# Moving TensorE's bias additions ahead in its written order, and fewer zero products between them

## The chip, the cores and the metric

The kernel runs on one core of one Trainium2 chip. A core has five engines that run side by side and meet only at semaphores: TensorE (PE in the profile) multiplies matrices, VectorE (DVE) and ScalarE (ACT) work elementwise, GpSimd (POOL) issues most of the loads here, and SyncE (SP) issues stores and a few loads. TensorE writes into PSUM, which this kernel uses as four "pairs" of two banks each. The metric is the time of one execution on the device in microseconds (us), as a median over runs.

## The reference

There are 8 batches of 576 tokens. The first part is attention with 8 heads of 64, a window of 128 tokens and a linear distance bias per head; the second mixes tokens with a small hypernetwork.

```python
scores = scale * np.matmul(q, k.transpose(0, 1, 3, 2))
bias = slopes[:, None, None] * (-np.abs(rel).astype(np.float32))[None, :, :]
mask = (rel >= 0) & (rel < window)
scores = np.where(mask, scores + bias[None], -1000000000.0)
attn = np.exp(scores - np.max(scores, axis=-1, keepdims=True))
attn = attn / (np.sum(attn, axis=-1, keepdims=True) + 1e-09)
x = np.matmul(attn, v)            # heads side by side: 576 x 512 a batch
wq, wk = x @ w_q, x @ w_k         # 576 x 64 each
W_tok = scale * np.einsum('bsd,btd->bst', wq, wk)
mixed = np.einsum('bst,btd->bsd', W_tok, x)
out = np.maximum(mixed, 0.0) @ w_out
```

## The kernel before

**Tiles.** A batch has four groups of key blocks (128 tokens each; the last group also takes the tail of 64), and each group two units `u` of four heads. Batches are handled in pairs from the mixing stage on.

**Names.** The work is cut into named operations, each with its batch and part:

- `Lq`, `Lk`, `Lv`, `Lt`: loads by GpSimd of a block of 128 tokens of q, k or v, or of the tails of two batches (lines 387 to 402). `LF` loads the first blocks on other queues. `Lw` and `Lwo` load the weights on SyncE (lines 449 to 461), behind `wz`, a small memset on VectorE (line 447).
- `TQ` (`TF`, `TJ` in batch 0): TensorE transposes a block of q and k into PSUM. `ETQ`, `EF`, `EJ` copy it out. `TT` and `ETT` do the tails.
- `QK`: scores of one group and unit into one pair, products over 64 rows. `EXP`: ScalarE's exponential of that pair into SBUF (line 613).
- `BI`: two products over 128 rows that write the logarithmic bias, mask included, into the pair, onto which `QK` then adds. This is so for the twelve units of batches 0 and 1, groups 0 to 2 (`PEB`). For the others `MUL` multiplies the exponentials by the exponential of the bias on VectorE (line 620).
- `PV`: exponentials times values, with the row sums. `RC` and `X`: VectorE's reciprocal and normalisation (lines 677 and 663). `XT`: transposes of the result.
- `WK`, `WQ`, `WT`, `G`, `MX`, `OUT`: the mixing stage and the output products; `EO` and `DO` copy and store.
- `WM.i`: `WARM[i]` products of zeros by zeros (128 x 128 by 128 x 256) into a bank that nobody reads. They have no effect on the output.

**Order.** The order of all work is one written list, `ORDER`. A word such as `BI0.2.0:P1` gives operation, engine and place in PSUM: P is TensorE, A ScalarE, D VectorE, G GpSimd, S SyncE; `P1` is pair 1 whole, `P01` bank 1 of pair 0. Each engine works through its words in their order. Dependencies and the reuse of buffers and banks become semaphore waits. So an operation that waits holds up all that stands behind it on its engine. The unit's bias is the operation that takes the pair; the scores follow into the same pair, and the exponential frees it:

```python
        if added:
            own = add("BI", b, f"{g}.{u}", w - 0.5, pe(0.43), [mkg[u], idh], eb, banks=2)
            s = add("QK", b, f"{g}.{u}", w, pe(0.225), [own, *need], em, mode=1)
        x = add("EXP", b, f"{g}.{u}", w + 0.6, {"ACT": (0.92, 1.02)}, [s, *oldp], ex, frees=[own])
```

The numbers in these calls are notes of the list's making; they play no part when the list is followed.

Of the kernel before, what the change touches and what calls it, by code (L numbers as in the profile page):

```python
# [47 lines left out]
WARM = (13, 3, 3, 8, 12, 2, 1, 8, 4, 11, 4, 3, 5, 5, 2, 2, 3)  # L48
# [4 lines left out]
WM.1:P10 TF0.1.0:P01 EF0.0.0:D TF0.0.1:P20 EF0.1.0:A WM.2:P10 Lq0.3:G ones:D EF0.0.1:A  # L53
TF0.1.1:P21 BI0.0.0:P1 EF0.1.1:A BI0.0.1:P3 Lk1.3:G QK0.0.0:P QK0.0.1:P EXP0.0.0:A TJ0.1.1:P20
TJ0.2.0:P21 Lq1.3:G EXP0.0.1:A WM.3:P10 Lk0.2:G EJ0.2.0:D zeros:D EJ0.1.1:A BI0.1.0:P0 Lk1.2:G
BI0.1.1:P1 QK0.1.0:P biasl:D QK0.1.1:P TT0:P20 Lq1.2:G EXP0.1.1:A TJ0.3.0:P21 WM.4:P30 Lk0.3:G
EXP0.1.0:A ETT0:D EJ0.3.0:D Lk1.1:G ETT1:D TQ1.3:P00 WM.5:P30 Lq1.1:G ETQ1.3:D TJ0.2.1:P01
WM.6:P10 EJ0.2.1:D BI0.2.1:P3 Lv0.1:G QK1.3.1:P2 BI0.2.0:P1 QK0.2.1:P EXP1.3.1:A QK0.2.0:P
QK1.3.0:P0 Lv0.0:G EXP1.3.0:A MUL1.3.1:D TQ1.2:P20 Lq1.0:G WM.7:P21 ETQ1.2:D EXP0.2.1:A Lv0.2:G
MUL1.3.0:D BI1.2.1:P0 TJ0.3.1:P20 EXP0.2.0:A QK1.2.1:P Lk1.0:G EJ0.3.1:D WM.8:P30 EXP1.2.1:A  # L60
QK0.3.1:P2 BI1.2.0:P3 Lv0.3:G QK0.3.0:P1 QK1.2.0:P EXP0.3.1:A TQ1.1:P00 Lk2.1:G WM.9:P01
ETQ1.1:D EXP0.3.0:A Lq2.1:G MUL0.3.1:D EXP1.2.0:A PV0.1:P1 Lv1.2:G MUL0.3.0:D BI1.1.0:P2
BI1.1.1:P0 QK1.1.0:P RC0.1:D QK1.1.1:P Lv1.3:G X0.1:D EXP1.1.0:A PV0.0:P3 RC0.0:D PV0.2:P1
Lk2.2:G X0.0:D EXP1.1.1:A WM.10:P20 RC0.2:D Lv1.1:G X0.2:D PV0.3:P3 WM.11:P20 RC0.3:D Lq2.2:G
TQ1.0:P10 X0.3:D XT0.0:P11 ETQ1.0:A Lk2.3:G TQ2.1:P30 EXT0.0:D XT0.1:P31 Lq2.3:G WM.12:P20
EXT0.1:A PV1.3:P1 Lv1.0:G BI1.0.0:P2 BI1.0.1:P0 QK1.0.0:P RC1.3:D QK1.0.1:P Lk2.0:G X1.3:D
WM.13:P31 EXP1.0.1:A ETQ2.1:D PV1.2:P1 Lv1.4:G EXP1.0.0:A WM.14:P31 RC1.2:D Lq2.0:G wz:D
TQ2.2:P00 X1.2:D Lw:S WM.15:P31 ETQ2.2:D Lv0.4:G XT1.1:P01 Lwo.2:S Lwo.0:S WM.16:P31 EXT1.1:D
Lt1:G Lwo.1:S TQ2.3:P00 Lwo.3:S QK2.1.1:P1 ETQ2.3:D PV1.0:P2 EXP2.1.1:A PV1.1:P3 RC1.0:D Lk3.3:G
X1.0:D QK2.2.1:P0 QK2.2.0:P1 EXP2.2.1:A RC1.1:D Lq3.3:G X1.1:D PV1.4:P2 EXP2.2.0:A XT1.0:P30  # L70
RC1.4:D Lk3.0:G X1.4:D TQ2.0:P31 EXT1.0:A Lq3.0:G PV0.4:P0 ETQ2.0:D QK2.1.0:P1 CWQ:A Lk3.1:G
RC0.4:D QK2.0.1:P2 X0.4:D QK2.0.0:P3 EXP2.0.1:A Lq3.1:G MUL2.1.1:D XTT0:P00 WK0:P01 CW.2:A
EXTT0:D Lk3.2:G MUL2.2.0:D EXP2.0.0:A WT0:P00 pads:D WQ0:P20 EWK0:A EWT0:D EXP2.1.0:A CW.0:D
Lq3.2:G G0:P21 EWQ0:D CW.1:D TT2:P30 EG0:A MUL2.2.1:D Lt2:G ETT2:D MX0.0:P0 MX0.2:P1 RM0.0:A
RM1.0:D MX0.1:P2 RM1.1:A CW.3:D MX0.3:P0 RM0.1:A TQ3.3:P31 Lv2.3:G RM1.3:D RM0.3:A QK2.3.0:P2
# [96 lines left out]
def kernel(  # L172
# [55 lines left out]
    def two(bank):  # L228
        return pairs[bank[0]]
# [748 lines left out]
```

## Time and profile before

| | us |
|---|---|
| median of 3 runs (143.6 to 144.33) | 143.62 |
| the profiled execution | 143.94 |
| its span, first to last instruction | 142.2 |
| TensorE busy | 135.0 |
| ScalarE busy | 116.3 |
| VectorE busy | 113.8 |
| GpSimd busy | 95.6 |

TensorE's 89 zero products are counted in its busy time. Busy times of matmuls overlap, since they are pipelined. The lines that the prediction shows are copied from the profile: an instruction line gives its start, its length, engine, source line, operation, what it writes and reads, how many, and in square brackets the idle time before it with what ended it. All matmuls stand at lines 250 and 253, which are helpers, so the tiles tell them apart: `warm` is a zero product, `blog,identh` a bias, `qkT` scores, `identh,nat` a transpose of q and k, `vt,pt` a `PV`.

### The profile page before, as it was taken

Reading aid. Unit: us, or ns where it says so; the run is one execution under the profiler, and the core shown is the slowest. Engines: PE = TensorE matmul, PEld = TensorE weight load, DVE = VectorE, ACT = ScalarE, POOL = GpSimd, SP = SyncE. Lnnn points to the kernel's source line nnn. Section 1 sums busy time; section 2 is a strip of 40 time slices with the busy share of each in tenths; the row PEclk is TensorE's granted clock in tenths of the full one; section 3 lists DMA queues with packets and bytes.
Section 4 is the critical chain, followed back from the end, with each engine's and each line's share of the span. In section 5 each row is a group of like instructions: output and inputs, shape, how many; then the busy total and the mean of one; then the engine's idle time right before and its main releaser. Section 6 shows DMA issues by size and latency. Waiting matters only on the chain.

```text
span 142.2 us, 4683 instructions
## 1 busy us (share of the span) xinstructions
PE 135.0 (95%) x1933; PEld 91.1 (64%) x1933; DVE 113.8 (80%) x269; ACT 116.3 (82%) x165; POOL 95.6 (67%) x118
## 2 busy tenths in 40 slices
PE   7999999999998999999999999999999999999980
PEld 5857657877763654689855448678765658763440
DVE  4976547766899999999879999999999999737240
ACT  4875496654997899999999999999999997968530
POOL 7999999999948969999989469999660000000000
PEclk9999999999999999999999999999999999999999
DMA  4999999999999999999999999999999955312694
GB/s 100 202 142 143 151 150 153 154 156 151 208 275 154 157 157 154 155 192 157 236 157 222 292 163 154 200 157 186 262 181 155 331 203 231 142 74 52 183 360 150
DMA packets 119478, 25.60 MB, mean 180 GB/s; under 512 B 114209, under 2 KB 114465, under 8 KB 119457
## 3 DMA queue, kind: packets, MB, share of 16 engines
q0 software_dynamic: 109264, 13.77, 152.9%
q1 hardware_dynamic: 9136, 11.28, 23.7%
q10 hardware_dynamic: 1056, 0.26, 0.8%
q8 instruction: 15, 0.25, 0.7%
q14 instruction: 7, 0.05, 0.1%
HBM read 29.62 MB, written 9.44 MB: 275 GB/s over the span
## 4 chain that ended last, share of the span: by engine, by line
PE 75%; ACT 14%; DVE 5%; issue 3%; DVEq 0%; ACTq 0%
PE pair L250 60%; PE pair L253 16%; ACT pt L613 10%; ACT rm L810 2%; DVE x L663 1%; DVE qkT L259 1%; DVE osb L259 1%; ACT wqT L257 1%; ACT xT L257 1%; DVE inv L677 1%; DVE xtl L663 0%; ACT gs L257 0%; ACT wkt L257 0%; DVE xTt L259 0%; DVE warm L300 0%
## 5 line engine op out<-in xcount | busy, mean ns | idle before, releaser
L613 ACT ACTIVATE pt<-pair 128x1024 f16<-128x1024 f32 x64 | 62.2, 1036 | 10.0 <-PE pair L250 9.8
L401 POOL DMA_DIRECT2D vt<-in_v_dram x40 | 35.1, 911 | 6.4 <-DMA nat<-in_q_dram 3.1
L250 PE MATMUL pair<-wout_sb,rm 128*128 128x512 f16 (+1 forms) x132 | 31.2, 373 | 0.0
L388 POOL DMA_DIRECT2D nat<-in_k_dram x31 | 29.6, 962 | 1.1 <-PE pair L253 1.1
L388 POOL DMA_DIRECT2D nat<-in_q_dram x30 | 29.0, 973 | 1.0 <-DMA nat<-in_k_dram 0.7
L620 DVE TENSOR_TENSOR pt<-pt,bias 128x1024 f16<-128x1024 f16 x36 | 23.6, 685 | 0.6 <-ACT pt L613 0.5
L250 PEld LDWEIGHTS <-pt 128*128 128x128 f16 x576 | 20.9, 97 | 4.0 <-issue 1.2
L250 PE MATMUL pair<-vt,pt 128*128 128x65 f16 x576 | 22.8, 193 | 0.0
L663 DVE TENSOR_TENSOR x<-pair,inv 128x512 f16<-128x512 f32 x32 | 21.8, 688 | 0.8
L250 PE MATMUL pair<-qkT 64*128 64x256 f16 (+2 forms) x320 | 21.0, 250 | 0.0
L259 DVE COPY qkT<-pair 128x1024 f16<-128x1024 f16 (+1 forms) x29 | 16.6, 593 | 5.2 <-PE pair L253 4.9
L250 PEld LDWEIGHTS <-rm 128*128 128x128 f16 x132 | 11.5, 98 | 12.3 <-issue 1.3
L253 PE MATMUL pair<-identh,nat 128*128 128x128 f16 x244 | 18.5, 219 | 0.1
L250 PEld LDWEIGHTS <-qkT 64*128 64x128 f16 x320 | 11.0, 94 | 9.8 <-issue 4.6
L257 ACT COPY osb<-pair 128x512 f32<-128x512 f32 x26 | 14.7, 622 | 3.0 <-PE pair L250 3.0
L253 PEld LDWEIGHTS <-nat 128*128 128x128 f16 x244 | 14.6, 98 | 3.3 <-issue 1.9
L250 PE MATMUL pair<-warm 128*128 128x256 f16 x89 | 14.2, 299 | 1.5 <-DVE warm L300 1.1
L259 DVE COPY osb<-pair 128x512 f32<-128x512 f32 (+1 forms) x11 | 7.1, 641 | 6.8 <-PE pair L250 6.1
L257 ACT COPY xT<-pair 128x1024 f16<-128x1024 f16 x11 | 10.9, 1013 | 1.9 <-PE pair L253 1.9
L620 DVE TENSOR_TENSOR pt<-pt,biasl 128x1024 f16<-128x1024 f16 x16 | 10.6, 687 | 1.4 <-ACT pt L613 1.3
L257 ACT COPY qkT<-pair 128x1024 f16<-128x1024 f16 (+1 forms) x12 | 10.7, 925 | 1.2 <-PE pair L253 1.2
L250 PEld LDWEIGHTS <-warm 128*128 128x128 f16 x89 | 8.8, 106 | 3.4 <-DVE warm L300 1.1
(71 smaller groups left out, 154.3 us busy)
## 6 DMA issues: line engine op xcount, KB each, us to landing
out_dram<-osb SPq DMA_DIRECT2D x31, 256.0 KB, 3.2
vt<-in_v_dram POOLq DMA_DIRECT2D x32, 128.0 KB, 6.4
nat<-in_k_dram POOLq DMA_DIRECT2D x31, 128.0 KB, 5.8
nat<-in_q_dram POOLq DMA_DIRECT2D x30, 128.0 KB, 6.1
out_dram<-osb SPq DMA_DIRECT2D x10, 128.0 KB, 2.6
osb<-in_moe_w_out_dram SPq DMA_DIRECT2D x4, 256.0 KB, 6.5
osb<-in_q_dram SPq DMA_DIRECT2D x4, 128.0 KB, 3.2
natt<-in_q_dram POOLq DMA_DIRECT2D x4, 128.0 KB, 5.5
```

Of the source, the lines that this page charges most:

```text
L250: hold(nc.tensor.matmul(*a, **k))
L253: hold(nc.tensor.transpose(*a))
L257: hold(nc.scalar.copy(out_ap, in_ap))
L259: hold(nc.vector.tensor_copy(out=out_ap, in_=in_ap))
L388: return lambda: nc.gpsimd.dma_start(out=natv(b, j, n), in_=(q, k)[j][b, :, P * n:P * n + P, :].transpose([1, 0, 2]))
L401: return lambda: nc.gpsimd.dma_start(out=vtv(b, t)[:n, :, 0:D], in_=v[b, :, P * t:P * t + n, :].transpose([1, 0, 2]))
L613: nc.scalar.activation(out=pt[:, 0:1024], in_=two(own.bank).rearrange("p e c -> p (e c)"), func=AF.Exp, scale=SCALE)
L620: ENG2[o.eng].tensor_tensor(out=pt[:, 0:1024], in0=pt[:, 0:1024], in1=bt, op=ALU.mult)
L663: nc.vector.tensor_tensor(out=x[r].rearrange("p (g h d) -> p g h d", g=2, h=4), in0=sums(p)[r, :, :, 0:64], in1=box["inv"][r].unsqueeze(3) ...
L677: nc.vector.reciprocal(out=box["inv"][r], in_=sums(p)[r, :, :, 64])
L810: hold(nc.scalar.activation(out=out_ap, in_=in_ap, func=AF.Relu, scale=WSCALE))
```

## The change

The words of all engines but TensorE keep their order. In TensorE's list, within batches 0 and 1:

- `BI0.0.0` goes from behind the first transposes' end to the place right behind `TF0.0.0`; `BI0.2.1` and `BI0.2.0` go ahead of `TQ1.3`; `BI1.2.0` ahead of `QK0.3.1`; `BI1.1.0` and `BI1.1.1` ahead of `PV0.1`; `BI1.0.0` ahead of `PV0.3`; `BI1.0.1` ahead of `PV1.3`.
- The zero products go from 89 in 17 groups to 44 in 12 groups, and a new operation `WA.0` adds two zero products onto the pair that holds `BI0.2.1`, because every pair or bank is in use there.

The order on TensorE from the start to the second batch's first scores, with the number of zero products behind each `WM` and `WA`:

```
before: WMx13 TF0.0.0 WMx3 TF0.1.0 TF0.0.1 WMx3 TF0.1.1 BI0.0.0 BI0.0.1 QK0.0.0 QK0.0.1 TJ0.1.1 TJ0.2.0
  WMx8 BI0.1.0 BI0.1.1 QK0.1.0 QK0.1.1 TT0 TJ0.3.0 WMx12 TQ1.3 WMx2 TJ0.2.1 WMx1 BI0.2.1 QK1.3.1 BI0.2.0
  QK0.2.1 QK0.2.0 QK1.3.0 TQ1.2 WMx8 BI1.2.1 TJ0.3.1 QK1.2.1 WMx4 QK0.3.1 BI1.2.0 QK0.3.0 QK1.2.0 TQ1.1
  WMx11 PV0.1 BI1.1.0 BI1.1.1 QK1.1.0 QK1.1.1 PV0.0 PV0.2 WMx4 PV0.3 WMx3 TQ1.0 XT0.0 TQ2.1 XT0.1 WMx5
  PV1.3 BI1.0.0 BI1.0.1 QK1.0.0 QK1.0.1 WMx5 PV1.2 WMx2 TQ2.2 WMx2 XT1.1 WMx3 TQ2.3 (from here the same)
after:  WMx13 TF0.0.0 WMx1 BI0.0.0 TF0.1.0 TF0.0.1 WMx3 TF0.1.1 BI0.0.1 QK0.0.0 QK0.0.1 TJ0.1.1 TJ0.2.0
  WMx3 BI0.1.0 BI0.1.1 QK0.1.0 QK0.1.1 TT0 TJ0.3.0 BI0.2.1 BI0.2.0 TQ1.3 WMx2 TJ0.2.1 WAx2 QK1.3.1
  QK0.2.1 QK0.2.0 QK1.3.0 TQ1.2 WMx4 BI1.2.1 TJ0.3.1 QK1.2.1 BI1.2.0 QK0.3.1 QK0.3.0 QK1.2.0 TQ1.1
  WMx3 BI1.1.0 BI1.1.1 PV0.1 QK1.1.0 QK1.1.1 PV0.0 PV0.2 BI1.0.0 PV0.3 WMx3 TQ1.0 XT0.0 TQ2.1 XT0.1
  BI1.0.1 PV1.3 QK1.0.0 QK1.0.1 WMx5 PV1.2 WMx2 TQ2.2 WMx2 XT1.1 WMx3 TQ2.3 (from here the same)
```

The diff without the rewritten `ORDER`:

```diff
-WARM = (13, 3, 3, 8, 12, 2, 1, 8, 4, 11, 4, 3, 5, 5, 2, 2, 3)
+WARM = (13, 1, 3, 3, 2, 4, 3, 3, 5, 2, 2, 3)
+WARM_ADD = (('0.2.1', 2),)
...
+    biased = {}
+
+    def add_zeros(i, key, n):
+        def em(o):
+            for _ in range(n):
+                mm(two(biased[key].bank)[:, 0, 0:256], warm[:, 0:P], warm, start=False, stop=False)
+
+        add("WA", "", i, 0.0, pe(0.22 * n), [wmz, biased[key]], em)
...
-            own = add("BI", b, f"{g}.{u}", w - 0.5, pe(0.43), [mkg[u], idh], eb, banks=2)
+            biased[f"{b}.{g}.{u}"] = own = add("BI", b, f"{g}.{u}", w - 0.5, pe(0.43), [mkg[u], idh], eb, banks=2)
...
+    for i, (key, n) in enumerate(WARM_ADD):
+        add_zeros(i, key, n)
     plan = od.follow(ORDER)
```

More of the change, by code (lines that the diff above doesn't have):

```diff
@@ L52 @@
 LF0.1.0.0:S LF0.1.0.1:S Lq0.2:G bias:A blog.0:D Lk0.1:G idh:D TF0.0.0:P00 blog.1:D Lt0:G
[L53 to L75, printed above, removed]
@@ new lines @@
+EF0.0.1:A TF0.1.1:P21 BI0.0.1:P3 EF0.1.1:A Lk1.3:G QK0.0.0:P QK0.0.1:P EXP0.0.0:A TJ0.1.1:P20
+TJ0.2.0:P21 Lq1.3:G WM.3:P10 EXP0.0.1:A Lk0.2:G EJ0.2.0:D BI0.1.0:P0 zeros:D EJ0.1.1:A
+BI0.1.1:P1 Lk1.2:G QK0.1.0:P biasl:D QK0.1.1:P TT0:P20 Lq1.2:G EXP0.1.1:A TJ0.3.0:P21 Lk0.3:G
+EXP0.1.0:A ETT0:D BI0.2.1:P3 EJ0.3.0:D BI0.2.0:P1 Lk1.1:G ETT1:D TQ1.3:P00 WM.4:P21 Lq1.1:G
+ETQ1.3:D TJ0.2.1:P01 WA.0:P EJ0.2.1:D Lv0.1:G QK1.3.1:P2 QK0.2.1:P EXP1.3.1:A QK0.2.0:P
+QK1.3.0:P0 Lv0.0:G EXP1.3.0:A MUL1.3.1:D TQ1.2:P20 Lq1.0:G WM.5:P21 ETQ1.2:D EXP0.2.1:A Lv0.2:G
@@ new lines @@
+BI1.2.1:P0 MUL1.3.0:D TJ0.3.1:P20 EXP0.2.0:A QK1.2.1:P Lk1.0:G EJ0.3.1:D BI1.2.0:P3 EXP1.2.1:A
+QK0.3.1:P2 Lv0.3:G QK0.3.0:P1 QK1.2.0:P EXP0.3.1:A TQ1.1:P00 Lk2.1:G WM.6:P01 ETQ1.1:D
+EXP0.3.0:A BI1.1.0:P2 Lq2.1:G MUL0.3.1:D BI1.1.1:P0 EXP1.2.0:A PV0.1:P1 Lv1.2:G MUL0.3.0:D
+QK1.1.0:P RC0.1:D QK1.1.1:P Lv1.3:G X0.1:D EXP1.1.0:A PV0.0:P3 RC0.0:D PV0.2:P1 Lk2.2:G X0.0:D
+EXP1.1.1:A BI1.0.0:P2 RC0.2:D Lv1.1:G X0.2:D PV0.3:P3 WM.7:P00 RC0.3:D Lq2.2:G TQ1.0:P10 X0.3:D
+XT0.0:P11 ETQ1.0:A Lk2.3:G TQ2.1:P30 EXT0.0:D XT0.1:P31 Lq2.3:G BI1.0.1:P0 EXT0.1:A PV1.3:P1
@@ new lines @@
+Lv1.0:G QK1.0.0:P RC1.3:D QK1.0.1:P Lk2.0:G X1.3:D WM.8:P31 EXP1.0.1:A ETQ2.1:D PV1.2:P1 Lv1.4:G
+EXP1.0.0:A WM.9:P31 RC1.2:D Lq2.0:G wz:D TQ2.2:P00 X1.2:D Lw:S WM.10:P31 ETQ2.2:D Lv0.4:G
+XT1.1:P01 Lwo.2:S Lwo.0:S WM.11:P31 EXT1.1:D Lt1:G Lwo.1:S TQ2.3:P00 Lwo.3:S QK2.1.1:P1 ETQ2.3:D
+PV1.0:P2 EXP2.1.1:A PV1.1:P3 RC1.0:D Lk3.3:G X1.0:D QK2.2.1:P0 QK2.2.0:P1 EXP2.2.1:A RC1.1:D
+Lq3.3:G X1.1:D PV1.4:P2 EXP2.2.0:A XT1.0:P30 RC1.4:D Lk3.0:G X1.4:D TQ2.0:P31 EXT1.0:A Lq3.0:G
+PV0.4:P0 ETQ2.0:D QK2.1.0:P1 CWQ:A Lk3.1:G RC0.4:D QK2.0.1:P2 X0.4:D QK2.0.0:P3 EXP2.0.1:A
@@ new lines @@
+EXT4.1:D QK5.2.1:P2 Lv5.4:G QK5.1.1:P0 EXP5.2.1:A OUT2.2:P30 RC4.1:D Lv5.3:G X4.1:D EXP5.1.1:A
+MUL5.1.0:D QK5.3.1:P2 Lq7.1:G MX2.4:P1 TQ6.2:P31 MUL5.2.1:D EXP5.3.1:A TQ6.1:P00 Lk7.0:G
+MUL5.1.1:D OUT3.2:P01 RMT2:A ETQ6.2:D Lq7.0:G ETQ6.1:A PV4.4:P2 MUL5.3.1:D PV5.0:P1 RC4.4:D
+OUT3.4:P31 Lt3:G EO3.2:A RC5.0:D X4.4:D EO2.2:A PV5.1:P0 X5.0:D EO3.4:A XT4.0:P20 RC5.1:D
+Lq7.2:G DO3.4:S PV5.2:P3 X5.1:D EXT4.0:A QK6.0.1:P1 DO3.1:S RC5.2:D Lk7.2:G PV5.3:P0 X5.2:D
+DO2.0:S EXP6.0.1:A DO1.2:S XT5.0:P21 RC5.3:D Lv6.1:G X5.3:D PV5.4:P3 EXT5.0:A QK6.2.0:P1 RC5.4:D
```

107 lines of the change are left out of this document (53 added, 54 removed).

## The prediction

> **What bounds the kernel now.** I read the page first, then who waits for whom, then the instructions of single engines in order of time. The page's head, three of its rows of 40 slices (tenths busy) and its group of zero products:
>
> ```profile
> span 142.2 us, 4683 instructions
> PE 135.0 (95%) x1933; PEld 91.1 (64%) x1933; DVE 113.8 (80%) x269; ACT 116.3 (82%) x165; POOL 95.6 (67%) x118
> ...
> PE   7999999999998999999999999999999999999980
> ...
> DVE  4976547766899999999879999999999999737240
> ACT  4875496654997899999999999999999997968530
> ...
> L250 PE MATMUL pair<-warm 128*128 128x256 f16 x89 | 14.2, 299 | 1.5 <-DVE warm L300 1.1
> ```
>
> TensorE (PE) looks full in nearly every slice, but 89 of its products multiply zeros. In slices 4 to 10, about 11 to 36 us, VectorE and ScalarE are half empty. From about 50 us all three are full, so there the work is one block: it can begin earlier, but not shrink. The view of waits, for the first 50 us and then for GpSimd (POOL) over the whole span, gives microseconds in total, times, and the longest:
>
> ```profile
> ACT pt L613 <- PE pair L250: 9.4, 8, 2.0
> ...
> POOL vt L401 <- DMA nat<-in_q_dram: 3.1, 1, 3.1
> ...
> POOL nat L388 <- PE pair L253: 1.1, 1, 1.1
> ```
>
> ScalarE's exponentials wait 9.4 us for TensorE, so early on TensorE sets the pace. GpSimd, which issues the loads, waits only 1.1 us for TensorE and longer for its own earlier loads. So I take loads to land when they land now; that limits how far compute can run ahead.
>
> **The change, part by part.** Only TensorE's order changes. The four other queues keep theirs, so no DMA is moved past anything. Zero products go from 89 to 46, counting the two of WA.0 that are added onto a bias: 43 fewer. The prices, from TensorE's instructions in order of time (start, length, work):
>
> ```profile
> 4.66 0.85 PE L250 MATMUL pair<-warm 128*128 128x256 f16 x3
> 5.30 1.25 PE L253 MATMUL pair<-ident,osb 128*128 128x128 f32 x6
> ...
> 9.40 1.03 PE L250 MATMUL pair<-warm 128*128 128x256 f16 x8 [0.34 <-ACT pt L613]
> 10.27 1.03 PE L250 MATMUL pair<-blog,identh 128*128 128x512 f16 x4
> 11.22 0.61 PE L250 MATMUL pair<-qkT 64*128 64x256 f16 x8
> ...
> 12.46 1.47 PE L250 MATMUL pair<-warm 128*128 128x256 f16 x12
> 13.87 0.61 PE L253 MATMUL pair<-identh,nat 128*128 128x128 f16 x8
> ...
> 17.02 0.62 PE L253 MATMUL pair<-identh,nat 128*128 128x128 f16 x8
> ```
>
> A row's length includes the last product's latency, so I price from start to start: a zero product is (10.27-9.40)/8 = 0.109 us. Four bias products take 11.22-10.27 = 0.95 us; four of twice 0.109 would be 0.87, and I put the other 0.08 on the step from products over 128 rows to scores over 64. At the very start a zero product takes (5.30-4.66)/3 = 0.213 us: half speed.
>
> Step 1, up to the second transposes of batch 1 (TQ1.2). BI0.0.0 moves into the half-speed time: four times 0.213 instead of four times 0.109, 0.42 us more. Two zero products fewer there give 0.43 back. I estimate 0 to 0.2 us for the first scores. WM.3 falls from 8 products to 3, and it stands bare on the path: its pair comes free at about 9.4 and biases and scores follow it, so 5 x 0.109 = 0.55 us are gained. The 12 zero products at 12.46 (WM.4) are worth nothing, because TQ1.3 starts at 13.87 when ScalarE has read its pair (11.88+1.94 = 13.82):
>
> ```profile
> 11.88 1.94 ACT L613 ACTIVATE pt<-pair 128x1024 f16<-128x1024 f32 x2 [1.14 <-PE pair L250]
> ...
> 10.51 1.00 POOL L388 DMA_DIRECT2D nat<-in_q_dram  x1
> ...
> nat<-in_q_dram POOLq DMA_DIRECT2D x1, 128.0 KB, 6.2
> ```
>
> The two biases of group 2 go into that hole. BI0.2.0 needs pair 1, freed by the first of these two exponentials; what queues behind it, TQ1.3, waits for the second anyway, so this new wait is free. TQ1.3 comes 0.6 us earlier, but TQ1.2 does not: its query block (issued at 10.51, landing after 6.2) is there at 16.7. TQ1.2 moves from 17.02 to 16.75, a gain of 0.27 us, and TensorE idles about 1 us before it. The load is late next.
>
> Step 2, from TQ1.2 to the scores of batch 1's first group (QK1.0.0), carries the gain. The first row counts the zero products between 17 and 31.1 us (with shortest, median and longest duration in ns), the second is QK1.0.0:
>
> ```profile
> L250 PE MATMUL pair<-warm x35: 269/272/283, 17.5 to 29.6; 128*128 128x256 f16 x35
> ...
> 31.16 0.61 PE L250 MATMUL pair<-qkT 64*128 64x256 f16 x8
> ```
>
> The same six biases lie in this stretch before and after. Zero products fall from 35 to 10 (WM.5, WM.6, WM.7 with 4, 3 and 3), 25 x 0.109 = 2.73 us, and the new order has two changes fewer between 128-row and 64-row products, 2 x 0.08 = 0.16. Not all of it is real, as some zeros covered waits: PV0.2 must wait until VectorE has read PV0.1 from the same pair, and PV0.3 likewise. BI1.0.0 now covers the second; for the first I estimate 0.3 us. Net 2.6, and with the 0.27 QK1.0.0 moves by 2.9 us, to 28.3. The moved biases also hold their pairs longer (BI1.0.0 takes pair 2 four microseconds ahead of its scores), which costs nothing: no other work asks for pair 2 in between.
>
> Step 3, from QK1.0.0 on. The order and the zero products (5, 2, 2, 3) are as before, so everything shifts, unless a load holds it. The tightest here is the query block of TQ2.2:
>
> ```profile
> 24.51 1.01 POOL L388 DMA_DIRECT2D nat<-in_q_dram  x1
> ...
> nat<-in_q_dram POOLq DMA_DIRECT2D x1, 128.0 KB, 5.5
> ...
> 32.97 0.61 PE L253 MATMUL pair<-identh,nat 128*128 128x128 f16 x8
> ```
>
> 24.51+5.5 = 30.0, needed at 32.97: slack 2.96. The 2.9 pass.
>
> Step 4, what the earlier work triggers. A small VectorE memset behind batch 1's normalisation releases SyncE's loads of the weights (1.25 MB). They start about 3 us earlier and meet other loads of GpSimd's:
>
> ```profile
> 33.10 0.06 DVE L447 MEMSET osb<- 128x1 f32 x1
> ...
> 33.21 0.37 SPq L452 DMA_DIRECT2D osb<-in_moe_w_q_dram  x1
> ...
> 32.68 1.10 POOL L388 DMA_DIRECT2D nat<-in_k_dram  x1
> 33.55 1.11 POOL L388 DMA_DIRECT2D nat<-in_q_dram  x1
> ...
> nat<-in_k_dram POOLq DMA_DIRECT2D x1, 128.0 KB, 5.5
> ...
> nat<-in_q_dram POOLq DMA_DIRECT2D x1, 128.0 KB, 8.9
> ...
> 30.39 0.88 POOL L401 DMA_DIRECT2D vt<-in_v_dram  x1
> ...
> vt<-in_v_dram POOLq DMA_DIRECT2D x1, 64.0 KB, 4.8
> ...
> 38.84 0.65 PE L250 MATMUL pair<-vt,pt 128*128 128x65 f16 x16
> ```
>
> The load issued 0.5 us before the weights lands after the usual 5.5, the one 0.3 us behind them after 8.9. With the weights at about 30.3, the half-size load at 30.39 (Lv0.4, for PV0.4) falls between the two. It lands at 35.2 now and is needed at 38.84-2.9 = 35.9. Bounds for its delay: 0 and 8.9-5.5 = 3.4 us, so PV0.4 gains between 2.9 and 0.2 us. I take 1 us, nearer to the load just ahead, because only half as much data has to pass. PV0.4 then starts at 36.2: 2.6 us gained.
>
> Step 5, the full block. Here every load must land at least that much before its use. The thinnest slack that I find after 50 us is at PV5.3:
>
> ```profile
> 86.57 1.58 POOL L401 DMA_DIRECT2D vt<-in_v_dram  x2
> ...
> vt<-in_v_dram POOLq DMA_DIRECT2D x1, 128.0 KB, 6.2
> ...
> 95.66 0.66 PE L250 MATMUL pair<-vt,pt 128*128 128x65 f16 x16
> ```
>
> The second of the two starts at about 87.2 and lands at 93.4: slack 2.25 us. So of the 2.6 us at most about 2.25 reach the end. Nothing after it depends on a load, so the tail shifts whole. Sum: 2.2, less 0.2 for small waits that I cannot see = 2.0 us. The profiled execution took 143.94 us with its 142.2 us span, 0.32 above the median of 143.62; 141.94 against it is 141.6 against the median.
>
> **The rivals.** (a) The weights catch Lv0.4 in full: gain 0.2 to 1.2 us, 142.4 to 143.4. For it speaks that this load is issued with the weights or just behind them. (b) Loads move with compute, as TensorE and the stores free their buffers earlier: gain 2.9, 140.7. Against it: GpSimd waits for landings, hardly for TensorE. (c) The zeros were hidden anyway: if the 16.7 us load pins all that follows, only 0.27 us stay, 143.4. Against it: ScalarE's 9.4 us of waiting for TensorE. (d) Slower: TensorE's clock falls. Its place is 13.3 to 16.75 us, where the new order leaves about 1.4 us idle in 3.4, some 60% busy, the thinnest stretch. At the start the half speed lasted from 1.06 to about 6 us, so one fall costs about 5 us at half speed, 2.5 us of work, exactly where TensorE sets the pace; with it the gain shrinks to about 0, and from the second fall on the kernel is slower: about 2.5 us more, 144.5 to 146. What stands against it is the tail, in stretches of time (length, busy time of PE, PEld, DVE, ACT and POOL, granted clock, DMA share, GB/s):
>
> ```profile
> 135.86:139.28 3.42, 2.10 (x14) 1.16 (x12) 1.54 (x3) 0.75 (x2) 0.00 (x0) 1.00 0.92 355
> 139.28:142.20 2.92, 0.00 (x0) 0.00 (x0) 0.00 (x0) 0.00 (x0) 0.00 (x0) 1.00 0.28 95
> ```
>
> A stretch that is 61% busy, and 2.9 empty microseconds after it, leave the clock at 1.00. [...]
>
> **How the numbers follow.** Forecast (gain 1.3 to 2.6): 0.60. (a) 0.16, a little over half of it beyond 0.5%. (b) 0.07. (c) 0.05. (d) 0.12. About 0.5% (0.7 us) is what a measurement of this kernel can tell from no change. Faster: 0.60+0.07+0.09 = 0.76; within: 0.07 of (a), 0.05 of (c) and 0.01 of (d) = 0.13; slower 0.11. The range 140.7 to 143.4 takes in (b) and (a) and leaves out (d); the forecast's own range is 141.0 to 142.3.
>
> **What would show it.** Right: 46 zero products, TQ1.2 still at 16.7 with about 1 us idle before it; QK1.0.0 near 28.3; the exponentials' wait for TensorE in the first 50 us well below 9.4; the memset of line 447 near 30.2; PV0.4 near 36.2; PV5.3 near 93.4, directly after its load. Wrong: a granted clock below 1.00 or zero products 0.213 us apart after 13 us (d); PV0.4 not before 38 (a); QK1.0.0 after 30 (c).

## The result, and the profile after

The changed kernel takes 142.24 us (median of 6 runs, 141.85 to 143.5) against 143.74 for the kernel before (6 runs, 143.6 to 144.33): a ratio of 0.9897, 95% interval 0.9856 to 0.9939. So it is about 1% faster. Later, on another occasion beside the experiments, it was 0.9907 (0.9884 to 0.993). The forecast was 141.6 us with a range of 140.7 to 143.4. The ratios here and below leave out a kernel's runs that took over 1.5% longer than its fastest (one each of e3, e8 and e9, four of e7's ten, three of e12's four), while the medians take in all runs.

The page of the changed kernel's profiled execution (142.39 us): the span, busy time with share and instructions, the chain of work that ended last by engine, and the exponentials' row with their idle time and its releaser.

```profile
span 140.5 us, 4597 instructions
...
PE 131.6 (94%) x1890; PEld 88.0 (63%) x1890; DVE 114.3 (81%) x269; ACT 116.5 (83%) x165; POOL 95.5 (68%) x118
...
PE 47%; ACT 15%; DMA 12%; POOL 12%; DVE 7%; issue 5%; DVEq 0%
...
L623 ACT ACTIVATE pt<-pair 128x1024 f16<-128x1024 f32 x64 | 62.1, 1039 | 6.8 <-PE pair L251 6.6
```

The last two of these lines, in the kernel before:

```profile
PE 75%; ACT 14%; DVE 5%; issue 3%; DVEq 0%; ACTq 0%
...
L613 ACT ACTIVATE pt<-pair 128x1024 f16<-128x1024 f32 x64 | 62.2, 1036 | 10.0 <-PE pair L250 9.8
```

The exponentials wait 6.6 us for TensorE instead of 9.8. No transfer stood on the chain before. Now 24% of it is DMA and the engine that issues loads. The kernel has got nearer to its loads.

TensorE's timeline of the changed kernel at the places that the prediction named (start, length, engine, line, operation, count, idle time before it and what ended it):

```profile
16.62 0.61 PE L254 MATMUL pair<-identh,nat 128*128 128x128 f16 x8 [0.35 <-ACT pt L623]
...
28.45 0.61 PE L251 MATMUL pair<-qkT 64*128 64x256 f16 x8
...
36.18 0.65 PE L251 MATMUL pair<-vt,pt 128*128 128x65 f16 x16
...
82.17 0.61 PE L251 MATMUL pair<-vt,pt 128*128 128x65 f16 x15 [0.36 <-DMA vt<-in_v_dram]
...
93.92 0.73 PE L251 MATMUL pair<-vt,pt 128*128 128x65 f16 x16
```

These are TQ1.2, QK1.0.0, PV0.4, the rest of PV4.2, and PV5.3. The "lead" of an operation is its start less its start in the trace of before, so negative is earlier; "end" is TensorE's last product:

| | TQ1.3 | TQ1.2 | QK1.0.0 | PV0.4 | TQ3.3 | TQ4.2 | OUT2.0 | PV5.3 | end |
|---|---|---|---|---|---|---|---|---|---|
| lead, us | -0.22 | -0.40 | -2.71 | -2.66 | -2.72 | -2.45 | -1.92 | -1.73 | -1.66 |

The whole gain is made by 28.45 us, holds to 61 us, and 1.0 us of it is given back between 61 and 94 us: 0.3 by TQ4.2, 0.5 at PV4.2 and 0.2 at TQ6.2. At the largest step, PV4.2, the store and load engines' timelines and the DMA view of the loads issued around 71.6 us (KB of one, median us from issue to landing) show, in the changed kernel:

```profile
70.17 2.35 SPq L910 DMA_DIRECT2D out_dram<-osb  x5
...
69.88 2.63 POOL L411 DMA_DIRECT2D vt<-in_v_dram  x3 [0.21 <-issue]
...
vt<-in_v_dram POOLq DMA_DIRECT2D x2, 128.0 KB, 10.5
```

and in the kernel before, for the same loads, issued around 71 us:

```profile
69.20 2.78 POOL L401 DMA_DIRECT2D vt<-in_v_dram  x3
...
vt<-in_v_dram POOLq DMA_DIRECT2D x2, 128.0 KB, 7.8
```

Five stores of 256 KB, which before stood behind these loads (72.61 to 75.36 us), have come forward with the work and now go out beside them. Lv4.2 takes 10.5 us instead of 7.8 and lands at 82.13 instead of 78.72. The remaining 0.7 us is the issue: GpSimd starts this load at 71.61 instead of 70.93 us, although PV4.2, which needs it, has come 2.4 us forward. PV4.2 needs the load at 81.81 us, so by these numbers either part alone (82.13 less 0.7, or less 2.7) would have left it without a wait.

### The profile page after: what moved, and what is told of

It reads as the page before. It is cut to its first block, busy times and chain, and to the rows that moved or that the text cites. A ratio compares the mean times of both kernels' runs of the same rounds, so it can differ in the third digit from the quotient of the medians.

```text
span 140.5 us, 4597 instructions
## 1 busy us (share of the span) xinstructions
PE 131.6 (94%) x1890; PEld 88.0 (63%) x1890; DVE 114.3 (81%) x269; ACT 116.5 (83%) x165; POOL 95.5 (68%) x118
## 4 chain that ended last, share of the span: by engine, by line
PE 47%; ACT 15%; DMA 12%; POOL 12%; DVE 7%; issue 5%; DVEq 0%
PE pair L251 37%; ACT pt L623 11%; PE pair L254 10%; POOL nat L398 8%; DMA nat<-in_k_dram 8%; DMA nat<-in_q_dram 4%; POOL vt L411 3%; ACT rm L820 2%; DVE x L673 2%; DVE qkT L260 2%; DVE pt L630 1%; DVE osb L260 1%; DVE inv L687 1%; ACT xT L258 1%; ACT wqT L258 1%
## 5 line engine op out<-in xcount | busy, mean ns | idle before, releaser
L251 PE MATMUL pair<-vt,pt 128*128 128x65 f16 x576 | 23.3, 193 | 0.5 <-DMA vt<-in_v_dram 0.4
L820 ACT ACTIVATE rm<-pair 128x512 f16<-128x512 f32 x19 | 9.8, 626 | 0.5 <-PE pair L251 0.5
L251 PE MATMUL pair<-warm 128*128 128x256 f16 x46 | 8.7, 318 | 1.4 <-DVE warm L301 1.1
```

The source lines that it names most:

```text
L251: hold(nc.tensor.matmul(*a, **k))
L820: hold(nc.scalar.activation(out=out_ap, in_=in_ap, func=AF.Relu, scale=WSCALE))
```

## The experiments

The table gives each kernel's median and ratio to the kernel before, and the leads in its traced execution. The second column is the time of the trace's first record of the clock, from which TensorE runs at full speed; before it products stand twice as far apart (0.213 and 0.109 us in the prediction), though the views print 1.00 there too. It matters further down. The kernel before, run beside these, had medians of 143.76 to 144.02 us.

| kernel | full clock at | QK1.0.0 | PV0.4 | TQ3.3 | PV5.3 | end | median us (range, runs) | ratio, 95% |
|---|---|---|---|---|---|---|---|---|
| before | 6.16 | 0 | 0 | 0 | 0 | 0 | | 1 |
| changed | 7.02 | -2.71 | -2.66 | -2.72 | -1.73 | -1.66 | 142.24 (141.85-143.5, 6) | 0.9897, 0.9856-0.9939 |
| e1 | 4.60 | -1.29 | -1.29 | -0.48 | -0.45 | -0.44 | 142.92 (142.62-143.59, 10) | 0.9945, 0.9922-0.9967 |
| e2 | 4.73 | -1.13 | -1.07 | -1.12 | -1.09 | -1.10 | 143.25 (142.51-144.13, 10) | 0.9962, 0.9931-0.9993 |
| e3 | 6.87 | -3.23 | -2.98 | -3.02 | -2.74 | -2.30 | 142.46 (141.75-143.9, 5) | 0.9932, 0.9881-0.9983 |
| e4 | 6.92 | -2.77 | -2.71 | -2.47 | -2.47 | -2.47 | 141.59 (141.29-143.12, 4) | 0.9862, 0.9803-0.9922 |
| e5 | 6.94 | +0.4 | +0.4 | +0.4 | +0.4 | +0.40 | 144.19 (143.53-144.56, 10) | 1.0009, 0.999-1.0028 |
| e6 | 6.23 | -3.11 | -2.98 | -1.92 | -1.92 | -1.92 | 142.02 (141.53-143.18, 4) | 0.988, 0.9834-0.9927 |
| e7 | 5.09 | -3.61 | -2.77 | -1.09 | -0.89 | -0.89 | 142.78 (141.58-144.35, 10) | 0.9873, 0.9844-0.9901 |
| e8 | 6.55 | -2.94 | -2.88 | -2.63 | -2.63 | -2.63 | 141.87 (141.19-146.98, 6) | 0.9846, 0.9818-0.9875 |
| e9 | 6.03 | -3.20 | -2.84 | -1.58 | -1.51 | -1.51 | 142.51 (141.65-144.16, 6) | 0.9885, 0.9853-0.9918 |
| e10 | 6.90 | -2.78 | -2.72 | -2.77 | -2.74 | -2.51 | 142.54 (141.75-142.59, 5) | 0.9907, 0.9884-0.993 |
| e11 | 5.95 | -2.81 | -2.76 | -1.40 | -1.36 | -1.36 | 141.78 (141.63-143.61, 7) | 0.9849, 0.9828-0.987 |
| e12 | 4.28 | -3.36 | +1.19 | +2.76 | +2.79 | +2.79 | 146.25 (142.85-146.63, 4) | none |

### Which part earns the gain: zeros alone (e1), biases alone (e2), no zeros (e3)

e1 keeps the order of before and takes only the zero products out:

```diff
-WARM = (13, 3, 3, 8, 12, 2, 1, 8, 4, 11, 4, 3, 5, 5, 2, 2, 3)
+WARM = (13, 1, 3, 3, 12, 2, 1, 4, 1, 2, 1, 1, 1, 5, 2, 2, 3)
```

> The order of before, with 32 zero products taken out: two of the three behind TF0.0.0, five of the eight ahead of BI0.1.0, and 25 of the 35 between TQ1.2 and QK1.0.0; no bias moves. Theory (zero products lay on the path, and most of the gain is theirs): 25 x 0.109 = 2.7 us are taken out of the stretch, but here the biases stay behind the waits that the zeros covered (BI1.1.0 and BI1.1.1 0.87 us behind PV0.1, BI1.0.0 and BI1.0.1 0.87 us behind PV1.3), so QK1.0.0 starts 1.2 to 1.5 us before its 31.16, at 29.7 to 30.0, and the time falls by 1.0 to 1.4 us against before, near the change's own 1.5 us, because the loads behind 60 us take the change's surplus away anyway. Rival (the gain is in the moved biases, the zeros filled waits): QK1.0.0 not before 30.8, time within 0.4 us of before.

e2 has the new order, with 32 zeros put back into its groups:

```diff
-WARM = (13, 1, 3, 3, 2, 4, 3, 3, 5, 2, 2, 3)
+WARM = (13, 3, 3, 8, 2, 12, 11, 12, 5, 2, 2, 3)
```

> The order of the change with its moved biases and its WA.0, but 32 zero products put back into its groups: WM.1 3, WM.3 8, WM.5 12, WM.6 11, WM.7 12. Theory (the zeros carry the gain): 0.2 to 0.7 us faster than before, QK1.0.0 at 30.4 to 30.9. Rival (the moved biases carry it): the 1.5 us of the change, QK1.0.0 near its 28.45.

e3 has the new order and only the 13 zeros at the very start:

```diff
-WARM = (13, 1, 3, 3, 2, 4, 3, 3, 5, 2, 2, 3)
-WARM_ADD = (('0.2.1', 2),)
+WARM = (13,)
+WARM_ADD = ()
```

> The change with all zero products gone but the first 13: 33 fewer. Theory (holes of about a microsecond do not cost TensorE its clock, and the loads set the end): clock 1.00, QK1.0.0 0.3 to 0.9 us before the change's 28.45, PV0.4 held by its load near 36, and the time within 0.3 us of the change, 1.3 to 1.8 us under before. Rival (the remaining zeros hold the clock): the clock falls in the stretch from 12 to 17 us, score products there take about double, and the time is 1 to 5 us above the change.

Between TQ1.2 and QK1.0.0 the lead grows by 2.31 us in the changed kernel (from 0.40 to 2.71), by 0.70 with the zeros out alone (0.59 to 1.29) and by 0.25 with the biases moved alone (0.88 to 1.13). Each part alone is worth little; together they give more than twice their sum. This stretch lies behind the clock's rise, and its length repeats: 14.14 us in both traces of the order and zeros of before (before, e5), 11.82 to 12.25 in the ten of the changed order whose zeros were not put back. The leads at QK1.0.0 themselves do not compare so well, since e1 and e2 reached full speed 1.4 to 1.6 us earlier than before; that is also why e2's QK1.0.0, at 30.03, lies ahead of what was expected. The times alone would not show that the parts need each other: e1 gains 0.55% (0.8 us, where 1.0 to 1.4 were expected) and e2 0.38%, together 0.93%, and the change 0.93 to 1.03%. The 0.55% has the zeros ahead of BI0.1.0 in it, and the change gives some of its gain back later. What TensorE waits for between 13.2 and 31 us says why the stretch behaves so. In e1 (line waited from, releaser, total us, times, longest):

```profile
PE pair L250 <- ACT pt L613: 1.0, 1, 1.0
PE pair L250 <- DVE x L663: 0.3, 1, 0.3
```

and in the changed kernel:

```profile
PE pair L254 <- ACT pt L623: 0.9, 3, 0.3
PE pair L251 <- DVE qkT L260: 0.2, 1, 0.2
```

With the zeros gone and the biases in their old place, PV0.1 stands 0.99 us idle until its pair is free: ScalarE reads it for EXP0.3.0 until 22.14 us. PV0.3 stands idle another 0.28 until VectorE has read its pair. The zeros had stood in front of these waits. The moved biases are real work in the same holes, and behind the holes they no longer stand in the path. PV0.1 starts at 22.17 us in the changed kernel and at 22.19 in e1, as the same exponential frees its pair just before (22.07 and 22.14); but in e1 four biases still stand between it and QK1.0.0, in the changed kernel only two. Neither half does that alone.

In e1 a second loss, 0.8 us between PV0.4 and TQ3.3, eats much of what was gained: the first product of line 250 with the weights waits 0.23 us for their conversion by ScalarE, since the weights' second load lands only at 39.20 us, and a later product waits 0.51 us for ScalarE's copy of the result, which stands behind the conversion.

e3 shows which of the remaining 33 zeros cost something: with the full clock at nearly the same time as in e10 (the changed kernel again; 6.87 and 6.90 us) QK1.0.0 comes 0.45 us earlier without them. But the first scores, QK0.0.0, are already 0.45 us earlier (7.58 and 8.03), so the four zeros ahead of them make the whole difference, and the 17 between them and QK1.0.0 cost nothing: without them TensorE waits. In e3's trace the clock stays at full up to the end of the work. Its median does not differ from the changed kernel's by more than the intervals allow. One of its five runs took 143.9 us with a mean clock of 0.983, the lowest in it; it has no trace, so whether the zeros that are left guard the clock in some runs is open.

### Where the gain goes behind 60 us: smaller stores (e4, e5), loads and stores in another order (e6, e7, e8)

e4 is the changed kernel, e5 the kernel before, with 32 of the 512 columns stored for batches 0 to 3:

```diff
+            w = 32 if b < 4 else c1 - c0
...
-                gated(nc.sync.dma_start(out=out[b, P * st:P * st + P, c0:c1], in_=osb))
+                gated(nc.sync.dma_start(out=out[b, P * st:P * st + P, c0:c0 + w], in_=osb[:, 0:w]))
```

> The change, with the stores of the batches 0 to 3 cut to 32 of 512 columns: the rest of these batches' output is left out, the computation is whole. Theory (the 1.0 us lost between 61 and 96 us goes to loads that the stores, moved ahead with the work, delay): Lv4.2 lands well ahead of PV4.2, OUT2.0 and PV5.3 keep at least 2.4 us of lead over before, and the time is 2.3 to 2.8 us under before, 0.7 to 1.2 under the change. Rival (loads are bound by GpSimd's issue at 0.87 us each, stores or not): the lead at PV5.3 stays at 1.7 us and the time at the change's.

> Before, with the stores of the batches 0 to 3 cut to 32 of 512 columns: the rest of these batches' output is left out. Theory (before, every load landed 2.25 us or more ahead of its use, so compute did not feel the stores): within 0.4 us of before. Rival (fewer stores speed up anything that loads, whatever the order on TensorE): 0.7 us or more faster.

With small stores the lead stays at -2.47 from 44 us to the end, and the DMA view of e4 shows the loads of the same block, Lv4.2 among them, at half the time:

```profile
vt<-in_v_dram POOLq DMA_DIRECT2D x2, 128.0 KB, 5.7
```

In the kernel before, the same cut is worth nothing (1.0009, 0.999 to 1.0028), so the stores cost nothing there. In the changed kernel's first trace they take part in what is given back: TensorE's one idle time from 60 to 100 us is PV4.2's 0.36 us for its load, and e4's trace shows none. But that is not the stores alone. In e10, the same kernel with the same stores at nearly the same time (69.87 to 71.80 us), Lv4.2 takes 10.2 us as well, and still the lead is -2.74 up to 100 us: GpSimd had issued the load at 70.54 and not at 71.61, so that it landed at 80.70, in time. The stores use up the slack; whether TensorE then waits hangs on when GpSimd issues, and that differs between two runs of one kernel. In time e4's gain over the changed kernel is not clear of the intervals either (0.9803 to 0.9922 against 0.9856 to 0.9939).

e6 leaves the stores alone and issues GpSimd's loads in the order in which TensorE needs them, from Lv2.3 on; the words of one stretch:

```diff
-Lk5.0 Lk5.1 Lq5.0 Lk5.2 Lq5.1 Lk5.3 Lq5.3 Lq5.2 Lv4.0 Lk6.0 Lv4.1 Lv4.3 Lv4.2 Lq6.0 Lq6.3 Lk6.3
+Lk5.1 Lq5.1 Lk5.0 Lq5.0 Lk5.3 Lq5.3 Lk5.2 Lq5.2 Lv4.1 Lv4.2 Lv4.3 Lk6.0 Lq6.0 Lv4.0 Lk6.3 Lq6.3
```

> The change, with GpSimd's loads from Lv2.3 on in the order in which TensorE needs them (Lv4.2 from the thirteenth to the tenth place of its run, Lq4.2 ahead of Lk4.3, Lq6.2 ahead of Lq6.1, Lk7.1 behind Lv5.4, and so on). Theory (single late loads take the lead away): the waits at TQ4.2 (0.2 us), OUT2.0 (0.5) and TQ6.2 (0.2) shrink, 0.2 to 0.7 us faster than the change, 1.7 to 2.2 under before. Rival (the sum of transfers is late, not their order): within 0.2 us of the change.

e7 puts ten stores of batches 0 to 3 further back in SyncE's list:

```diff
-GT3.0 DO0.3 GT3.2 DO1.4 GT4.0 DO1.3 GT4.1 DO1.0 DO0.1 DO0.2 GT4.2 DO0.0 DO1.1 GT5.2 GT4.3 GT5.3
+GT3.0 GT3.2 DO1.4 GT4.0 DO1.3 DO0.3 GT4.1 GT4.2 GT5.2 GT4.3 DO1.0 DO1.1 DO0.2 DO0.1 DO0.0 GT5.3
```

> The change, with stores moved back on SyncE's queue: DO0.3 behind DO1.3, the five stores of 70 us behind the gate GT4.3 (about 78 us), the four of 93 us behind GT7.0 (about 101 us). Theory (stores that run into loads take the lead away): Lv4.2 and Lk6.3 land 2 to 4 us earlier, but Lq6.2 lands as before near 88.6 and holds TQ6.2, so 0 to 0.3 us faster than the change. Rival (the stores do not matter): Lv4.2 stays at 82.1.

e8 does both.

> The change, with the loads' order and the stores' places of the two runs before this one together. Theory: what either leaves is covered by the other; 0.5 to 1.0 us faster than the change, 2.0 to 2.5 under before (141.2 to 141.7 us). Rival (transfers are late in sum): within 0.2 us of the change.

In e6 Lv4.2 lands at 74.96, in e8 at 75.76 us, and in both the lead does not change any more behind TQ3.3 (about 45 us). That fits the same cause: with the stores whole and the needed loads first, nothing is lost there. It does not prove it, since e10 loses nothing there either. In e7 Lv4.2 lands at 78.89, 3.2 us earlier than in the changed kernel, as expected. In time e8 is 2.2 us under before (0.9846), within the 2.0 to 2.5 expected; e6 and e7 are not clear of the changed kernel, and e7's median is 0.5 us above its 142.24. e7's lead is flat behind 50 us too, but 2.5 us were lost before that, in another place: between QK1.0.0 (-3.61) and TQ3.3 (-1.09).

### The earlier place: the weights' loads against Lv0.4 (e9 to e12)

TensorE's timeline of e7 at PV0.4:

```profile
36.07 0.19 PE L250 MATMUL pair<-vt,pt 128*128 128x65 f16 x1
37.99 0.61 PE L250 MATMUL pair<-vt,pt 128*128 128x65 f16 x15 [1.73 <-DMA vt<-in_v_dram]
```

The load is Lv0.4, issued at 30.23 us as always, but landing at 37.95. This is rival (a) of the prediction. In e7 the weights' loads began at 29.66 us, 0.89 earlier than in the changed kernel's trace, because the whole front of that run was earlier; and it was earlier since the clock had risen at 5.09 us instead of 7.02. Ordered by the weights' start (in e1, e2 and e5 the weights go out behind 31.9 us, and Lv0.4 lands between 34.95 and 35.33):

| kernel | weights issued | Lv0.4 issued | Lv0.4 landed | idle in PV0.4 |
|---|---|---|---|---|
| before | 33.21 | 30.39 | 35.17 | 0 |
| e11 | 31.77 | 30.22 | 35.27 | 0 |
| changed | 30.55 | 30.21 | 35.85 | 0 |
| e4 | 30.49 | 30.26 | 36.44 | 0.2 |
| e10 | 30.48 | 30.22 | 35.68 | 0 |
| e8 | 30.32 | 30.33 | 36.05 | 0 |
| e6 | 30.15 | 30.22 | 36.80 | 0.8 |
| e9 | 30.07 | 30.33 | 37.31 | 1.16 |
| e3 | 30.03 | 30.31 | 36.02 | 0 |
| e7 | 29.66 | 30.23 | 37.95 | 1.73 |
| e12 | 28.96 | 30.28 | 39.92 | late with TQ2.0 |

e9 was to hold back the four loads of the output weights by a second small memset (here in e8's kernel):

```diff
+            wz2 = add("wz2", "", "", next(i), DVE(0.06), [],
+                      lambda o: nc.vector.memset(wide32(0)[:, 0:1], 0.0))
...
-                lwo = add("Lwo", "", c, next(i), {"SP": (0.9, 5.0)}, [wz], lambda o, c=c: nc.sync.dma_start(
+                lwo = add("Lwo", "", c, next(i), {"SP": (0.9, 5.0)}, [wz2], lambda o, c=c: nc.sync.dma_start(
```

The new memset stands behind EXT1.1 on VectorE, and the conversions CW.2, CW.0 and CW.1 a few places later.

> The version with loads in order of use and the stores moved back, and in addition the four loads of the output weights (1 MB of the 1.25 MB) held back by a second memset behind EXT1.1, about 2 us after the first; the conversions CW.2, CW.0 and CW.1 stand a little later in their lists. Theory (the weights' loads, brought forward by the change, take Lv0.4's bandwidth, and what they cost depends on how early the front of a run is): PV0.4 no longer waits for Lv0.4 in its middle, the lead at PV0.4 equals that at QK1.0.0 within 0.2 us, and at the end it is still 2.6 to 3.0 us; median 141.3 to 141.7 us, and no run far above. Rival 1 (the two small loads of the projection weights, which stay where they are, do it alone): no change against the version without the memset, 141.9 us. Rival 2 (the output weights now come late themselves): a wait for the conversions ahead of OUT1.3 or a late exponential behind CW.2, 0.5 to 1.5 us lost between 38 and 46 us, 142.5 us or more.

e10 is the changed kernel again.

> The changed kernel itself, beside the version with later weights and on the same chip. If the moment at which TensorE reaches full speed sets the start of a run, and the rest follows from it: with a rise at 4.6 to 5.1 us the scores QK1.0.0 come 3.0 to 3.6 us ahead of the kernel before, but Lv0.4 lands too late and PV0.4 gains at most 2.8; with a rise near 7 us the leads are as in the first profile of it (2.7 and 2.66). Either way the end is 1.2 to 1.9 us ahead and the median 141.9 to 142.4 us. If the phase of the rise meant nothing, the leads would not follow it.

e11 and e12 move the first memset itself in e8's kernel, later and earlier:

```diff
 e11, VectorE:  -RC1.2 wz X1.2 ETQ2.2 EXT1.1
                +RC1.2 X1.2 ETQ2.2 wz EXT1.1
 e12, VectorE:  -RC1.3 X1.3 ETQ2.1 RC1.2 wz X1.2
                +RC1.3 X1.3 wz ETQ2.1 RC1.2 X1.2
```

> The version with loads in order of use and stores moved back; alone the memset that releases the weights' loads goes behind ETQ2.2, so that all six loads start about 1.2 us later (31.3 to 31.5 instead of 30.3) and Lv0.4, issued at 30.3, is a full microsecond ahead of them. Theory (Lv0.4 is late when the weights are issued with it or ahead of it): Lv0.4 lands by 35.8 whatever the front of the run does, PV0.4 does not wait for it, the lead at PV0.4 is that at QK1.0.0 within 0.1 us; if the weights themselves are not late for CWQ (before 37.5), the end is 2.6 to 3.0 us ahead and the median 141.3 to 141.8 us. Rival 1 (Lv0.4's landing hangs on the loads of GpSimd's own queue and not on the weights): it still lands at 36 to 38 us, and the time is that of the version without the move, 141.9 us or, in a run with an early rise of the clock, 142.5. Rival 2 (the later weights become the wait): CWQ or CW.2 comes 0.5 to 1.2 us late, WK0 or the exponentials behind it lose as much, 142.3 us or more.

> The same with the memset one place earlier than in that version, ahead of ETQ2.1, so that the weights start about 0.9 us earlier (29.4) and Lv0.4 is 0.9 us behind them. Theory: Lv0.4 lands at 37.5 to 38.5, the middle of PV0.4 waits 1.2 to 2 us for it, and the end is only 0.9 to 1.6 us ahead: median 142.5 to 143.0 us. Rival 1 (the weights do not matter for it): Lv0.4 lands as without the move and the median is 141.7 to 142.0 us; TensorE even gains where the weights' conversions come earlier.

e9 missed its aim: the memset touches only the buffer of Lwo.0, and Lwo.2, which goes first, did not wait for it (issued at 31.03, the next at 32.18). So it does not test what its text says; in its trace the collision is there in full.

e10's front came out as expected for a late rise: full clock at 6.90 us, leads of 2.78 and 2.72, no wait in PV0.4. Its end did not: the traced run kept 2.51 us instead of 1.2 to 1.9, and the median, 142.54, is a little above the 141.9 to 142.4 expected.

e12 is the plainest case. The weights started 1.36 us earlier than in e8 (about 0.4 of it from a front that is 3.36 us ahead at QK1.0.0 instead of 2.94, with the clock's rise at 4.28 us instead of 6.55), and Lv0.4 and also Lq2.0, issued just ahead of it, were 4 us late (39.15 instead of 35.02 for Lq2.0). TensorE's timeline of e12, the middle of PV1.4 and then TQ2.0:

```profile
35.23 0.61 PE L250 MATMUL pair<-vt,pt 128*128 128x65 f16 x15 [1.19 <-DMA vt<-in_v_dram]
...
35.69 0.61 PE L253 MATMUL pair<-identh,x 128*128 128x128 f16 x8
39.20 1.03 PE L253 MATMUL pair<-identh,nat 128*128 128x128 f16 x8 [2.90 <-DMA nat<-in_q_dram]
```

The loss was larger than expected, 146.25 us instead of 142.5 to 143.0, and the reason is a second one behind the first. The stretches of e12's time (length, busy time and count of PE, PEld, DVE, ACT and POOL, granted clock, DMA share, GB/s):

```profile
38.20:38.40 0.20, 0.00 (x0) 0.00 (x0) 0.00 (x0) 0.00 (x0) 0.00 (x0) 1.00 2.28 170
38.40:38.60 0.20, 0.00 (x0) 0.00 (x0) 0.00 (x0) 0.00 (x0) 0.00 (x0) 0.53 2.30 180
...
45.00:45.20 0.20, 0.20 (x10) 0.20 (x12) 0.00 (x0) 0.20 (x1) 0.20 (x2) 0.50 1.91 122
45.20:45.40 0.20, 0.20 (x10) 0.09 (x6) 0.04 (x1) 0.20 (x2) 0.20 (x2) 0.91 2.27 145
...
35.00:38.41 3.41, 1.06 (x23) 0.88 (x22) 0.91 (x2) 2.08 (x3) 1.31 (x2) 1.00 1.64 264
```

In the stall TensorE's clock falls at 38.41 us, and it stays at half until 45.24. From TQ2.0 at 39.20 to TQ3.3 at 49.47 e12 takes 10.27 us, before 8.32, so the half speed costs about 2.0 us, behind the 4 us of waiting itself (1.19 and 2.90). Two more of its runs, 146.2 and 146.3 us, have no trace. e8's one run of 146.98 us (mean clock 0.974, as in e12's traced run of 146.63 us) has no trace; it fits the same event, but this is not shown.

e11 is the other end. Lv0.4 lands at 35.27, as expected by 35.8, and PV0.4 does not wait. But in the traced run of 142.79 us rival 2 came true as well:

```profile
39.03 1.09 PE L250 MATMUL pair<-wqk_sb,xT 128*128 128x64 f16 x32 [0.78 <-ACT wqk_sb L257]
...
41.86 1.05 PE L250 MATMUL pair<-x,wk 128*64 128x512 f16 x8 [0.51 <-ACT wk L257]
```

The weights started only at 31.77 (the memset stands behind a copy that itself waits), and their conversion (wqk_sb) was late, and with it the copy (wk) behind it. Four of its seven runs lie between 141.63 and 141.78 us. Its ratio is 0.9849 (0.9828 to 0.987), clear of the changed kernel's 0.9907 (0.9884 to 0.993) on the same chip, though not of the 0.9856 to 0.9939 of the first comparison; the same holds for e8.

## Why the prediction was right, and where not

**Sum.** 2.0 us were forecast, 1.66 came at TensorE's last product in the trace and 1.5 between the medians. The place and the size of the front's gain were right; the mis-sized term is the cap of step 5.

**Step 1.** The first scores come 0.21 us later in the trace, but there the clock rises 0.86 us later than in before's, which costs 0.43 us at half speed; without that they are 0.2 us earlier (said: 0 to 0.2). TQ1.3 comes 0.22 us earlier, not 0.6, for the same reason. TQ1.2 starts at 16.62 (said: 16.75), but not for the reason given. The load that was to pin it was issued at 10.48 and landed at 15.14, not 6.2 us after its issue. What holds TQ1.2 is its pair, which ScalarE reads until 16.57, and the idle time before it is 0.35 us and not 1. In e7 TQ1.2 moves 1.35 us ahead, so there is no pin. One landing time from one trace was used as if it were a constant.

**Step 2.** 2.6 us were worked out from 25 zeros fewer; 2.31 came (11.83 us instead of 14.14 from TQ1.2 to QK1.0.0, which starts at 28.45, said 28.3). The counts hold: 46 zeros, 10 of them here. The reading was too simple, though. e1 takes as many zeros out of this stretch and gains 0.70, so a zero there was not worth 0.109 us by itself. The sum was right only because the moved biases fill the waits that the zeros had covered; "for the first I estimate 0.3 us" went to PV0.2, where e1 shows no wait, and passed over PV0.1's wait until ScalarE has read its pair, 0.99 us in e1. The prediction moved BI1.1.0 and BI1.1.1 into that hole without pricing it.

**Step 3.** Everything behind QK1.0.0 shifts; TQ2.2 passes.

**Step 4.** The memset of line 447 runs at 30.44 (said 30.2), Lv0.4 lands 0.68 us later than before (said 1), PV0.4 starts at 36.18 (said 36.2). That the two agree is luck: 36.2 was to be the landing of its load, but the load is there at 35.85 and holds nothing, and PV0.4 comes where the front's 2.7 us put it. Nor is the delay a fixed quantity: across the kernels of the table above it runs from 0.1 to 4.75 us, beyond the upper bound of 3.4, mostly according to when the weights start, and in the changed order that goes with the clock's rise (29.66 us for a rise at 5.09 in e7, 30.55 for 7.02 in the changed kernel; only e3, with 30.03 for 6.87, stands apart).

**Step 5.** "I take loads to land when they land now" failed. The thinnest slack was to leave 2.25 us; at PV5.3 the lead is 1.73, and PV4.2 waits for a load that in before's trace had landed at 78.72, 3.4 us earlier. The stores move with the work and lengthen the loads beside them (10.5 and 10.2 us with them, 5.9 in e4), and GpSimd's issues do not move ahead in this trace. The step treated a slack as a reserve although the change moves the other traffic as well. e10 shows that this is not the same each time: there Lv4.2 lands at 80.70, Lv5.3, whose slack was to be the cap, at 92.52 (before 93.41, first trace 94.00), and the lead is still -2.74 at PV5.3. "Nothing after it depends on a load" is wrong as well: in the trace of before 17 of GpSimd's loads land behind PV5.3's start, and in e10 PV6.1 waits 0.17 us and TQ7.3 0.43 us for theirs, at 104 and 106 us, which takes the lead to -2.51. What the untraced runs of it lost, the median of 142.54 against 141.75 in the traced one, no trace shows.

**The rivals.** (a) did not happen in the changed kernel's traces, but it is real: e7 and e9 show it, e12 at its worst. (b) did not happen in the first trace, where GpSimd issued Lv4.2 0.7 us later than before; in e10 it did in part: from 53 to 70 us GpSimd's issues come 1.2 to 1.8 us earlier than before, most of these loads land 0.6 to 1.4 us earlier, and 2.5 us of the 2.9 reach the end. (c) is refuted by QK1.0.0. (d) did not happen at its place: between 13.3 and 16.75 us the changed kernel is busier than was thought:

```profile
13.30:16.75 3.45, 2.58 (x44) 2.03 (x43) 1.55 (x5) 1.50 (x3) 3.45 (x5) 1.00 2.42 157
```

75% and not 60%, and the clock stays at 1.00. e3, without these zeros, tests it harder: from 13.69 to 17.11 us it is 62% busy, and the clock stays too (mean 1.0 over the traced run). But such a fall does happen in this program, in e12, 2.1 us after the end of the last product (35.69 + 0.61 = 36.30 to 38.41). In the 3.41 us before it TensorE was busy for 1.06 us, 31%. Before's tail with 61% (2.10 of 3.42 us) did not bring a fall, nor did a stretch in e7 with 49% (1.68 us from 35.81 to 39.22). Whether it is the busy share that decides, and where it would between 31% and 49%, these few stretches do not show. The 0.12 for (d) was the author's estimate; before's trace shows the clock at 1.00 to the end of its work.

## What to carry to other kernels

A filler in an engine's list costs its price only where nothing else would hold up the work behind it. Here 25 fillers taken out alone gave 0.70 us, since the waits that they covered appeared; with real work from further down put into the holes it was 2.31. When work moves ahead, list which transfers it triggers and which loads these will run beside, because a slack read from the old trace assumes the old traffic. Where the slack of loads has been used up, as here, one trace is a sample: two traces of the changed kernel gained 1.66 and 2.51 us at their end.

## What the runs showed of the hardware that was not expected

**The clock's steps.** In all the traces the time at full clock is a whole multiple of 3.413 us: 133.12 us in the changed kernel's, 39 times that, 136.53 in before's, 40 times, and 39 or 40 in the others; in e12 it is 10 at full, 2 at half, 29 at full. These steps do not count from the program's start: the rise comes between 4.28 and 7.02 us, with the same 13 zero products at the start. The six transposes behind the first biases show it, in e7 (rise at 5.09):

```profile
5.42 0.82 PE L253 MATMUL pair<-ident,osb 128*128 128x128 f32 x6
```

and in the changed kernel (rise at 7.02):

```profile
5.73 1.46 PE L254 MATMUL pair<-ident,osb 128*128 128x128 f32 x6
```

In before's order this shift goes through to the end: e5's trace rises 0.78 us later than before's, starts its scores 0.4 us later and ends 0.40 us later. In the changed order an early rise also brings the weights ahead of Lv0.4 (29.66 against 30.23 us in e7). The half speed from 1.06 us to a rise between 4.28 and 7.02 us costs an estimated 1.6 to 3.0 us, half of that time, which is 1 to 2% of 142; and a rise 1.93 us earlier makes 0.95 us at the first scores (0.21 in the changed kernel, -0.74 in e7), two thirds of the change's whole gain.

**Loads beside other traffic.** The 64 KB load Lv0.4 took 4.8 us with the weights issued 2.8 us behind it, 5.6 us with them 0.34 us behind, 7.7 us with them 0.57 us ahead, and 9.6 us with them 1.32 us ahead (before, changed, e7, e12). Between these there is no smooth line: with the weights from 0.26 us behind it to 0.28 ahead it took 5.5 to 7.0 us in no clear order (e10, e4, e8, e6, e9, e3), and why stays open.
